# Retention and two feed-forward layers on one Trainium2 core: two first-block products are computed inside the retention, with earlier slice conversion, a paired last group and an output scale spread by TensorE

## The chip, the cores and the metric

The kernel runs as one program on one core of a Trainium2 chip. The metric is the device time of one execution in microseconds; a smaller number is better. The engines are named as in the profile: PE is TensorE's matmul (PEld its weight load), DVE is VectorE, ACT is ScalarE, POOL is GpSimd, SP is SyncE, which issues most loads.

## The reference

Three steps follow each other. A retention: for each of 4 batches and 8 heads a state of 64 x 64 runs over 768 tokens,

```
state = gamma[h] * state + outer(k[t], v[t])
y[t]  = (1 / sqrt(64)) * (q[t] @ state)
```

Then y becomes x of 3072 tokens by 512, and two feed-forward layers with 2048 hidden units follow: `h = x @ w_in; x = (h * sigmoid(1.702 * h)) @ w_out`, and `h = x @ w_in2; out = relu(h)**2 @ w_out2`. Weights arrive as float64 words and are brought to pairs of float32 parts (a high part that TensorE multiplies in one pass, and a low part, the rest).

## The kernel before

**The retention.** The 3072 tokens are cut into 24 units of 128 (6 per batch). Unit u has two loads of 512 KB (`load_unit`, issued on SP, line 459; the second one is half as long for the last unit of a batch). Seven units are in flight; the load of unit u + 7 is issued when unit u's outputs are done. The work goes in groups, line 477: units 0 to 3 one by one, then pairs (4, 5) to (20, 21), then 22 and 23 one by one, so k runs from 0 to 15 with an empty last group. In the loop at line 632 each group k does, in program order:

- `scores` of its units (line 487, PE): products of q and k, 8 float32 products per unit, into the PSUM tags `sc0` or `sc1`, with the scaled v of the unit on POOL (line 504, `vs`);
- ScalarE's high part of a converted weight slice, if one is held (`cv_high`, line 163), and ScalarE's high part of x for the first block (`split_0`, line 516);
- `outputs` of group k - 1: `grow` adds to the state in `dp` (line 552), which ScalarE copies out (line 557); `within` (line 566) and `across` (line 581) give the outputs in PSUM tag `yp` (or `sc1` for units 1 and 22);
- DVE: the masks of group k (line 496, `pt`), the low part of x for the first block, in `cv_group` the low part of the held slice (line 168) and in groups 8, 10, 12, 14 the conversion of another one (`convert`: lines 142 and 148), and last `scaled`, the scaling of the outputs of group k - 1 by the table `ytab` (lines 603, 610, 613);
- POOL's issues of slice loads (`cv_load`, line 128, in groups 5, 7, 9, 10, 12, ...), ScalarE's scaling of a loaded slice (`cv_a`, line 136), and the loads of later units.

The scores of group k + 1 need the score bank that the masks of group k read; `within` needs the masks, and the `yp` bank that `scaled` of the group before has read. `sc0`, `sc1` and `yp` are one buffer of two banks each, `dp` two banks. Each engine works through its own list in order.

The output scale of batch chunk 0, `ytab_sb[0]`, is a load of 128 x 512 float32 (256 KB) on SP's queue between the two halves of unit 2 (line 627); ScalarE derives the other five from it (line 645). Ahead of unit 0 TensorE runs 9 warm-up products (line 475), behind unit 0's scores 6 more (`fill`, line 637).

**The first layer, first two blocks of 512 tokens.** For n = 0, 1 the loop at line 853 runs over 16 slices f: `up(n, f)` is 12 matmuls of 128 x 512 (lines 675 to 677) into PSUM tag `b{f % 4}`, then Gelu and a high copy on ScalarE (lines 684, 685) and the low part on DVE (line 689); `down(n, f - 2)` is 12 more into `b4` to `b7` (lines 712 to 714). During block 0 each `up` also converts 2, 2, 2 or 3 weight slices (`cv_step`), each with a high copy, a rounding and a low part, until all 32 are done. The PSUM pool `ps` of this stage (line 665) is opened when the retention's pool closes, and each of its tiles waits for the earlier tile in the same place (`reuse_waits="tile"`).

**The rest** runs the second half of the tokens and the second layer with a seven-product scheme for 2 x 2 blocks (line 893), for which `background` prepares weights on DVE, ScalarE and POOL; the change touches none of it.

Of the kernel before, what the change touches and what calls it, by code (L numbers as in the profile page):

```python
# [10 lines left out]
F32 = mybir.dt.float32  # L11
F32R = mybir.dt.float32r
# [3 lines left out]
ACTF = mybir.ActivationFunctionType  # L16
# [3 lines left out]
P = 128  # L20
# [25 lines left out]
BG0 = 4.5  # L46
BG1 = (4.9,) * 9 + (2.6,) * 5 + (2.8, 0.0)
PAUSE = 3.0
CVG = (8, 10, 12, 14)
RAWG = {5: 1, 7: 1, 9: 1, 10: 1, 12: 1, 13: 2, 14: 1, 15: 1}  # L50
FILL = 6
RAWS = 5
BGUP = (2.4, 2.75)
BGD = (0.6, 1.9)
# [11 lines left out]
def tile_retention_then_two_ffns(  # L66
# [90 lines left out]

    held = deque()

    def cv_high():  # L160
        if held:
            w, hm, key = held[0]
            nc.scalar.copy(out=w[:, :, 0], in_=hm.rearrange("p (k c) -> p k c", c=P))

    def cv_low():
        if held:
            w, hm, key = held.popleft()
            v.tensor_tensor(
                out=w[:, :, 1], in0=hm.rearrange("p (k c) -> p k c", c=P), in1=w[:, :, 0], op=ALU.subtract
            )  # L170
            ws[key] = w
# [13 lines left out]
    def cv_group(k):  # L185

        cv["step"] += 1
        cv_low()
        if k in CVG and cv["b"] < cv["a"]:
            convert()  # L190

    def cv_ahead(k):

        if k == CVG[-1] - 1:
            cv["ahead"] = RAWS
        for _ in range(RAWG.get(k, 0)):
            cv_load()
        n = cv["a"]
        if n < min(cv["load"], cv["b"] + 2) and cv["step"] >= loaded[n] + 2:
            cv_a()  # L200

    def cv_step(f=None):

# [213 lines left out]
    def split_x(n, src, t=None):  # L417
# [5 lines left out]
            v.tensor_tensor(out=lo, in0=x, in1=hi, op=ALU.subtract)  # L423
        hl[n] = t

    with tc.manual_schedule():

        with (
# [30 lines left out]
                    nc.sync.dma_start(out=units[u][i][:, a - 1024 * i:z - 1024 * i], in_=qkv[u, :, a:z])  # L459

            nc.scalar.dma_start(out=tab_sb, in_=tab)
            load_unit(0)
            warm_sb = att.tile([P, 512], BF16, tag="x0", name="warm_sb")
            nc.vector.memset(warm_sb, 0.0)
# [9 lines left out]
            for i in range(WARM):  # L474
                nc.tensor.matmul(warm[:, 0, :, :], warm_sb[:, 0:P], warm_sb, start=True, stop=True)

            groups = [(u,) for u in range(4)] + [(u, u + 1) for u in range(4, NU - 2, 2)] + [(NU - 2,), (NU - 1,)]
            second = {pair[1] for pair in groups if len(pair) > 1}

            def scores(u):  # L480
# [29 lines left out]
            def split_0():  # L510
# [14 lines left out]

                return low if blocks else None

            def banked(t):
                return t.rearrange("p (k b) i -> p b k i", b=2)

            def outputs(pair):

                tag = "sc1" if pair in ((1,), (NU - 2,)) else "yp"
                yp = aps.tile([P, 2, NP, P], F32, tag=tag, name=f"yp{pair[0]}", bufs=1)

                def views(u):
# [4 lines left out]
                def grow(u):  # L541

                    b, c = divmod(u, CPB)
                    if c == CPB - 1:
                        return
                    kn = views(u)[1]
                    vs = pend[u][1]
                    dp = state[b][0] if c else aps.tile([P, NP, D], F32, tag="dp", name=f"dp{b}")
                    for p in range(NP):
                        for a in range(2):  # L550
                            h = 2 * p + (a ^ p % 2)
                            nc.tensor.matmul(  # L552
                                dp[64 * a:64 * a + 64, p, :], kn[:, h, :], vs[:, h, :],
                                start=(c == 0 and p == 0), stop=(c == CPB - 2), skip_group_check=True,
                            )
                    ns = att.tile([P, NP, D], F32, tag="st", name=f"st{u}", bufs=3)
                    nc.scalar.copy(out=ns, in_=dp)
                    state[b] = (dp, ns)
                    snaps[u + 1] = ns
# [63 lines left out]
                return scaled  # L623

            load_unit(1)
            load_unit(2, (0, 1024))
            nc.sync.dma_start(out=ytab_sb[0], in_=ytab)
            load_unit(2, (1024, 2048))
            for u in range(3, UNITS):
                load_unit(u)  # L630

            for k, group in enumerate(groups + [()]):
                masks = [scores(u) for u in group]
                if k == 0:
                    fill = aps.tile([P, 2, NP, P], F32, tag="yp", name="fill", bufs=1)
                    for i in range(FILL):
                        nc.tensor.matmul(fill[:, 0, :, :], warm_sb[:, 0:P], warm_sb, start=True, stop=True)
                cv_high()
                low = split_0()
                before = groups[k - 1] if k > 0 else ()  # L640
                scaled = outputs(before) if before else None
                for u in group:
                    if 0 < u < CPB:
                        for p in range(NP):
                            nc.scalar.mul(ytab_sb[u][:, p, :], ytab_sb[0][:, p, :], ystep_sb[:, u, p:p + 1])
                for masked in masks:
                    masked()
                if low is not None:
                    low()
                cv_group(k)  # L650
                if scaled is not None:
                    scaled()
                cv_ahead(k)
                for u in before:
                    load_unit(u + UNITS)
# [8 lines left out]
            wpool[f] = wb_p  # L664
        ps_p = ctx.enter_context(tc.tile_pool(name="ps", bufs=1, space=PSUM, reuse_waits="tile"))

        gs = {}
        acc = {}

        def up(n, f):  # L670
            hi, lo = weights(f, 0)
            hp = ps_p.tile([P, TB], F32, tag=f"b{f % 4}", name=f"h{n}_{f}")
            for k in range(KD):
                xh, xl = hl[n][k]
                nc.tensor.matmul(hp, lo[:, k], xh, start=(k == 0), stop=False)  # L675
                nc.tensor.matmul(hp, hi[:, k], xh, start=False, stop=False)  # L676
                nc.tensor.matmul(hp, hi[:, k], xl, start=False, stop=(k == KD - 1))  # L677
            slots = [wr_p[i] for i in (EARLY, EARLY + 1 + 2 * (f % 2), EARLY + 2 + 2 * (f % 2))]
            g, gh, gl = (
                pool.tile([P, TB], t, tag="w", name=f"{name}{n}_{f}")  # L680
                for pool, t, name in zip(slots, (F32, F32R, F32R), ("gs", "gh", "gl"))
            )

            nc.scalar.activation(out=g, in_=hp, func=ACTF.Gelu_apprx_sigmoid)
            nc.scalar.copy(out=gh, in_=g)
            gs[n, f] = (gh, gl)

            def low():
                v.tensor_tensor(out=gl, in0=g, in1=gh, op=ALU.subtract)

            if n == 0 and cv["b"] < len(order):
                cv_step(low)
                for _ in range(1 + (f % 4 == 3)):
                    if cv["b"] < len(order):
                        cv_step()
            else:
                low()
                if n == NSTD - 1:
                    next(first_x, None)
                pace(n, f)  # L700
# [150 lines left out]
            fetch()  # L851

        for n in range(NSTD):
            for f in range(NF):
                up(n, f)
                if f >= LOOK:
                    down(n, f - LOOK)
# [285 lines left out]
def _tables():  # L1143
# [4 lines left out]
    vt = np.exp(-t[:, None] * lg[None, :]).reshape(CPB, P, H).transpose(1, 0, 2).reshape(P, CPB * H)  # L1148

    yt = np.exp(t[:P, None] * lg[None, :]) / np.sqrt(D)  # L1150
    yt = np.repeat(yt.reshape(P, NP, 2).transpose(2, 1, 0), D, axis=0)

    ys = np.exp(P * np.arange(CPB)[:, None] * lg[None, :])
    ys = np.repeat(ys.reshape(CPB, NP, 2).transpose(2, 0, 1).reshape(2, CPB * NP), D, axis=0)
# [69 lines left out]
```

## Time and profile before

| | us |
|---|---|
| median of 3 runs | 1023.68 (1023.49 to 1024.23) |
| profiled execution, its own time | 1023.72 |
| its span, first to last instruction | 1022.0 |
| PE busy | 1012.6 (99%) |
| DVE busy | 734.0 (72%) |
| ACT busy | 525.5 (51%) |
| POOL busy | 143.9 (14%) |
| retention: start to the first slice product | 80.70 |

The span is what the profile covers; the execution's own time is 1.7 us longer. PE is busy nearly all the time, so the waits of PE are what is left to look for, and the place to look is the retention, where its matmuls are short and depend on loads, masks and scalings. Busy shares of the other engines say only how much of their time is spoken for, not whether PE waits for them.

### The profile page before, as it was taken

Reading aid. Unit: us, or ns where it says so; the run is one execution under the profiler, and the core shown is the slowest. Engines: PE = TensorE matmul, PEld = TensorE weight load, DVE = VectorE, ACT = ScalarE, POOL = GpSimd, SP = SyncE. Lnnn points to the kernel's source line nnn. Section 1 sums busy time; section 2 is a strip of 40 time slices with the busy share of each in tenths; the row PEclk is TensorE's granted clock in tenths of the full one; section 3 lists DMA queues with packets and bytes.
Section 4 is the critical chain, followed back from the end, with each engine's and each line's share of the span. In section 5 each row is a group of like instructions: output and inputs, shape, how many; then the busy total and the mean of one; then the engine's idle time right before and its main releaser. Section 6 shows DMA issues by size and latency. Waiting matters only on the chain.

```text
span 1022.0 us, 15448 instructions
## 1 busy us (share of the span) xinstructions
PE 1012.6 (99%) x5551; PEld 838.4 (82%) x5551; DVE 734.0 (72%) x976; ACT 525.5 (51%) x815; POOL 143.9 (14%) x209
## 2 busy tenths in 40 slices
PE   8999999999999999999999999999999999999998
PEld 6988888888888888888888888888888888888886
DVE  5778897997566998566998576885455985446953
ACT  4126765444556565556565787563234463334433
POOL 2442222431111101211102210001000001000000
PEclk9999999999999999999999999999999999999999
DMA  9995766995999978999978999867766867766664
GB/s 354 407 368 179 277 226 253 363 362 209 372 358 356 334 270 271 405 377 351 349 249 271 399 401 306 273 209 240 211 194 194 275 213 246 204 194 195 211 191 144
DMA packets 119627, 287.65 MB, mean 281 GB/s; under 512 B 13056, under 2 KB 13184, under 8 KB 119296
## 3 DMA queue, kind: packets, MB, share of 16 engines
q1 hardware_dynamic: 90864, 181.71, 52.8%
q0 software_dynamic: 27968, 103.82, 27.7%
q10 hardware_dynamic: 720, 1.15, 0.3%
q8 instruction: 44, 0.72, 0.3%
q14 instruction: 31, 0.25, 0.1%
HBM read 213.23 MB, written 73.40 MB: 280 GB/s over the span
## 4 chain that ended last, share of the span: by engine, by line
PE 96%; DMA 2%; DVE 1%; ACT 0%; issue 0%; SPq 0%
PE D L893 37%; PE X L893 21%; PE Z L893 10%; PE Y L893 5%; PE h L675 3%; PE y L712 3%; PE h L677 3%; PE y L714 3%; PE h L676 3%; PE y L713 3%; DMA unit<-qkv 2%; PE yp L566 2%; PE sc L487 2%; PE yp L581 1%; PE dp L552 1%; DMA tab_sb<-tab 0%
## 5 line engine op out<-in xcount | busy, mean ns | idle before, releaser
L893 PE MATMUL D<-gx,r 128*128 128x512 f32 x1680 | 383.2, 389 | 0.0
L893 PEld LDWEIGHTS D<-gx,r 128*128 128x128 f32 x1680 | 314.9, 188 | 66.7 <-DVE gx L1012 1.4
L1012 DVE TENSOR_TENSOR gx<-g,gx 128x1024 fp32r<-128x1024 f32 x140 | 170.4, 1220 | 44.7 <-ACT gx L1011 44.2
L893 PE MATMUL X<-xh,r 128*128 128x512 f32 x640 | 197.3, 389 | 0.2 <-ACT g L911 0.2
L1011 ACT CAST gx<-g 128x1024 fp32r<-128x1024 f32 x140 | 145.5, 1051 | 89.8 <-PE D L893 83.0
L911 ACT COPY g<-X 128x512 f32<-128x512 f32 x120 | 70.1, 584 | 176.9 <-PE X L893 176.9
L916 DVE TENSOR_TENSOR g<-Z,g 128x512 f32<-128x512 f32 x80 | 55.1, 689 | 132.9 <-ACT g L911 98.2
L893 PEld LDWEIGHTS X<-xh,r 128*128 128x128 f32 x640 | 120.0, 188 | 25.7 <-ACT g L911 0.8
L893 PE MATMUL X<-xl,r 128*128 128x512 f32 x320 | 124.5, 389 | 0.0
L893 PE MATMUL Z<-xh,r 128*128 128x512 f32 x320 | 98.5, 389 | 0.0
L893 PEld LDWEIGHTS Z<-xh,r 128*128 128x128 f32 x320 | 60.1, 188 | 12.5
L893 PEld LDWEIGHTS X<-xl,r 128*128 128x128 f32 x320 | 60.1, 188 | 12.5
L893 PE MATMUL Z<-xl,r 128*128 128x512 f32 x160 | 62.2, 389 | 0.0
L336 POOL DMA_DIRECT2D kw<-wq x32 | 30.2, 944 | 196.9 <-DVE wq L335 144.0
L136 ACT ACTIVATE raw<-raw 128x384 f32<-128x384 f32 (+1 forms) x96 | 46.0, 514 | 8.5 <-DMA raw<-w 8.5
L675 PE MATMUL h<-hl,w 128*128 128x512 f32 x128 | 49.9, 390 | 0.0
L676 PE MATMUL h<-hl,w 128*128 128x512 f32 x128 | 49.8, 389 | 0.0
L677 PE MATMUL h<-hl,w 128*128 128x512 f32 x128 | 49.8, 389 | 0.0
L712 PE MATMUL y<-gh,w 128*128 128x512 f32 x128 | 49.8, 389 | 0.0
L713 PE MATMUL y<-gh,w 128*128 128x512 f32 x128 | 49.8, 389 | 0.0
L714 PE MATMUL y<-gl,w 128*128 128x512 f32 x128 | 49.8, 389 | 0.0
L893 PE MATMUL Y<-xh,r 128*128 128x512 f32 x160 | 49.3, 389 | 0.0
(100 smaller groups left out, 1354.2 us busy)
## 6 DMA issues: line engine op xcount, KB each, us to landing
r<-kw SPq DMA_DIRECT2D x560, 256.0 KB, 3.5
kw<-wq POOLq DMA_DIRECT2D x32, 896.0 KB, 7.3
unit<-qkv SPq DMA_DIRECT2D x44, 512.0 KB, 9.9
raw<-w POOLq DMA_DIRECT2D x32, 512.0 KB, 5.2
kw<-wh POOLq DMA_DIRECT2D x16, 1024.0 KB, 5.9
raw<-win POOLq DMA_DIRECT2D x16, 512.0 KB, 7.8
kw<-w POOLq DMA_DIRECT2D x16, 512.0 KB, 6.8
raw<-wout POOLq DMA_DIRECT2D x16, 512.0 KB, 8.8
```

The costliest lines, as they stand in the source:

```text
L136: nc.scalar.activation(out=hm[:, a:z], in_=raw[:, a:z, 1].bitcast(F32), func=ACTF.Prelu, scale=scale, alpha=-2.0 ** 32)
L675: nc.tensor.matmul(hp, lo[:, k], xh, start=(k == 0), stop=False)
L676: nc.tensor.matmul(hp, hi[:, k], xh, start=False, stop=False)
L677: nc.tensor.matmul(hp, hi[:, k], xl, start=False, stop=(k == KD - 1))
L712: nc.tensor.matmul(a, lo[:, e], gh, start=s0, stop=False)
L713: nc.tensor.matmul(a, hi[:, e], gh, start=False, stop=False)
L714: nc.tensor.matmul(a, hi[:, e], gl, start=False, stop=s1)
L893: nc.tensor.matmul(a, w, b, start=start, stop=stop, skip_group_check=True)
L911: nc.scalar.copy(out=t, in_=a)
L916: v.tensor_tensor(out=t, in0=a, in1=t, op=ALU.add)
L1011: nc.scalar.copy(out=hi, in_=src)
L1012: v.tensor_tensor(out=lo, in0=src, in1=hi, op=ALU.subtract)
```

## The change

- The output scale comes as 2 rows (a 2 x 128 selector beside the 2 x 512 scale, loaded on ScalarE's queue behind the mask table) and one product of TensorE in place of the six fill products spreads it over the partitions; ScalarE copies it out of PSUM. The 256 KB load on SP goes, and unit 2 is loaded like the others.
- Units 22 and 23 become a pair, so the retention has 14 groups and the empty one. The outputs of this last pair go to tag `sc0`.
- Slice loads begin in group 7 instead of 5; conversions are 1, 1, 2, 1, 2, 1 in groups 9 to 14 instead of one in groups 8, 10, 12 and 14, and nine slices are scaled by ScalarE within the retention. The high and low parts of held slices are made at the head of the group, ahead of the masks.
- In groups 10 and 11 the products of slices 0 and 1 of block 0 (`early_up`) run between the scores and the outputs, with Gelu, high copy and low part; the low part stands on DVE behind the masks and ahead of the conversions. `dp` has one bank, the product `hp` has the other.
- Block 0's loop starts at slice 2, and converts 2, 3, 2, 3, ... slices per `up`.

```diff
-CVG = (8, 10, 12, 14)
-RAWG = {5: 1, 7: 1, 9: 1, 10: 1, 12: 1, 13: 2, 14: 1, 15: 1}
-FILL = 6
+CVG = {9: 1, 10: 1, 11: 2, 12: 1, 13: 2, 14: 1, 15: 1}
+RAWG = {7: 1, 8: 1, 9: 2, 10: 1, 11: 2, 12: 2, 13: 2, 14: 1}
+EARLYUP = {10: 0, 11: 1}
...
         cv["step"] += 1
-        cv_low()
-        if k in CVG and cv["b"] < cv["a"]:
-            convert()
+        for _ in range(CVG.get(k, 0)):
+            if cv["b"] < cv["a"]:
+                convert()
...
-        if k == CVG[-1] - 1:
+        if k == 9:
             cv["ahead"] = RAWS
         for _ in range(RAWG.get(k, 0)):
             cv_load()
-        n = cv["a"]
-        if n < min(cv["load"], cv["b"] + 2) and cv["step"] >= loaded[n] + 2:
-            cv_a()
+        for _ in range(CVG.get(k + 1, 0)):
+            n = cv["a"]
+            if n < cv["load"] and cv["step"] > loaded[n]:
+                cv_a()
...
+    def product(hp, hi, lo, x):
+        for k in range(KD):
+            xh, xl = x[k]
+            nc.tensor.matmul(hp, lo[:, k], xh, start=(k == 0), stop=False)
+            nc.tensor.matmul(hp, hi[:, k], xh, start=False, stop=False)
+            nc.tensor.matmul(hp, hi[:, k], xl, start=False, stop=(k == KD - 1))
...
             nc.scalar.dma_start(out=tab_sb, in_=tab)
+            ysel = xy_p.tile([P, 2, TB], F32, tag="xy", name="ysel").rearrange("p a n -> p (a n)")[0:2, 0:P + NP * P]
+            nc.scalar.dma_start(out=ysel, in_=ytab)
...
-            groups = [(u,) for u in range(4)] + [(u, u + 1) for u in range(4, NU - 2, 2)] + [(NU - 2,), (NU - 1,)]
+            groups = [(u,) for u in range(4)] + [(u, u + 1) for u in range(4, NU, 2)]
...
+            def early_up(f):
+
+                if not spare:
+                    spare.append(wa_p.tile([P, 2, TB], F32, tag="w1", name="ge"))
+                hp = aps.tile([P, TB], F32, tag="hp", name=f"h0_{f}", bufs=1)
+                product(hp, *weights(f, 0), hl[0])
+                g = spare[0][:, f]
+                t = wa_p.tile([P, 2, TB], F32R, tag="w1", name=f"ghl{f}")
+                nc.scalar.activation(out=g, in_=hp, func=ACTF.Gelu_apprx_sigmoid)
+                nc.scalar.copy(out=t[:, 0], in_=g)
+                gs[0, f] = t[:, 0], t[:, 1]
+                return lambda: v.tensor_tensor(out=t[:, 1], in0=g, in1=t[:, 0], op=ALU.subtract)
...
-                tag = "sc1" if pair in ((1,), (NU - 2,)) else "yp"
+                tag = {(1,): "sc1", groups[-1]: "sc0"}.get(pair, "yp")
...
-            load_unit(2, (0, 1024))
-            nc.sync.dma_start(out=ytab_sb[0], in_=ytab)
-            load_unit(2, (1024, 2048))
-            for u in range(3, UNITS):
+            for u in range(2, UNITS):
                 load_unit(u)
...
-                    for i in range(FILL):
-                        nc.tensor.matmul(fill[:, 0, :, :], warm_sb[:, 0:P], warm_sb, start=True, stop=True)
-                cv_high()
+                    nc.tensor.matmul(fill[:, 1, :, :], ysel[:, 0:P], ysel[:, P:], start=True, stop=True)
+                    nc.scalar.copy(out=ytab_sb[0], in_=fill[:, 1, :, :])
+                for i in range(len(held)):
+                    cv_high(i)
+                while held:
+                    cv_low()
                 low = split_0()
+                if k in EARLYUP:
+                    low = early_up(EARLYUP[k])
...
-                for _ in range(1 + (f % 4 == 3)):
+                for _ in range(1 + f % 2):
...
-            for f in range(NF):
+            for f in range(0 if n else LOOK, NF):
```

## Rows read from the trace of the kernel before

**Rows 1.** Waits of PE: line, what for, us in total, times, longest:

```profile
PE sc L487 <- DMA unit<-qkv: 2.2, 3, 1.3
...
PE yp L581 <- issue: 1.0, 2, 0.6
```

**Rows 2.** Windows: PE, PEld, DVE, ACT, POOL busy, PE clock, DMA share, GB/s:

```profile
20.00:40.00 20.00, 18.76 (x368) 17.02 (x370) 13.56 (x25) 4.99 (x17) 8.65 (x11) 1.00 1.03 407
...
66.00:81.00 15.00, 15.00 (x316) 13.42 (x313) 12.69 (x18) 4.74 (x10) 5.93 (x8) 1.00 0.61 225
81.00:160.00 79.00, 79.00 (x350) 65.37 (x349) 68.01 (x117) 50.06 (x87) 19.63 (x34) 1.00 0.67 231
```

**Rows 3.** Chain that ended last, in the retention: start us, us, what:

```profile
26.32 0.61 PE dp L552 x16
...
29.71 1.99 PE sc L487 x32
...
57.87 0.60 issue
...
59.22 1.99 PE sc L487 x32
...
72.03 0.61 PE dp L552 x16
...
75.90 1.09 PE sc L487 x16
```

**Rows 4.** Timeline of PE up to unit 11: start us, us, and idle before:

```profile
1.20 4.02 PE L475 MATMUL warm<-warm_sb 128*128 128x512 bf16 x9 [1.20 <-DVE warm_sb L464]
...
6.41 1.47 PE L637 MATMUL fill<-warm_sb 128*128 128x512 bf16 x6
...
25.16 1.16 PE L487 MATMUL sc<-unit 64*128 64x128 f32 x16 [0.62 <-DMA unit<-qkv]
...
35.05 1.16 PE L487 MATMUL sc<-unit 64*128 64x128 f32 x16
36.65 1.16 PE L487 MATMUL sc<-unit 64*128 64x128 f32 x16 [0.43 <-DVE x L603]
```

**Rows 5.** The same chain at the first matmuls of slices 0, 1 and 2:

```profile
80.70 0.43 PE h L675
...
83.69 0.23 PE h L675
...
86.41 0.23 PE h L675
```

**Rows 6.** Timeline of DVE and POOL in groups 6, 10, 12 and 13:

```profile
31.12 2.34 DVE L496 TENSOR_TENSOR pt<-sc,tab_sb 128x1024 f32<-128x1024 f32 x2
...
53.87 2.34 DVE L496 TENSOR_TENSOR pt<-sc,tab_sb 128x1024 f32<-128x1024 f32 x2
...
69.02 1.19 POOL L504 TENSOR_TENSOR vs<-unit,tab_sb 128x512 f32<-128x512 f32 x1 [1.46 <-DVE pt L496]
69.34 1.46 DVE L148 SCALAR_TENSOR_TENSOR hm<-raw,hm 128x512 uint16<-128x512 uint16 x1
...
70.86 1.29 DVE L610 TENSOR_TENSOR xout<-yp,ytab 128x512 f32<-128x512 f32 x2
```

**Rows 7.** DVE's groups by form, 0 to 82 us: busy us, mean ns:

```profile
L148 DVE SCALAR_TENSOR_TENSOR hm<-raw,hm 128x512 uint16<-128x512 uint16 x5 | 4.5, 890 | 0.2
...
L168 DVE TENSOR_TENSOR w<-hm,w 128x512 fp32r<-128x512 f32 x4 | 2.7, 683 | 0.1
L142 DVE TENSOR_SCALAR hm<-raw 128x512 uint32<-128x512 uint32 x5 | 2.1, 418 | 0.0
```

**Rows 8.** Timeline of DVE and ACT at the end of the retention:

```profile
80.80 0.68 DVE L610 TENSOR_TENSOR xout<-yp,ytab 128x512 f32<-128x512 f32 x1
...
84.43 0.62 ACT L685 CAST gh<-gs 128x512 fp32r<-128x512 f32 x1
85.09 0.69 DVE L689 TENSOR_TENSOR gl<-gs,gh 128x512 fp32r<-128x512 f32 x1 [2.49 <-ACT gh L685]
```

More of the change, by code (lines that the diff above doesn't have):

```diff
@@ L158, in tile_retention_then_two_ffns, with cv_high @@
     held = deque()
-    def cv_high():
+    def cv_high(i=0):
         if held:
-            w, hm, key = held[0]
+            w, hm, key = held[i]
             nc.scalar.copy(out=w[:, :, 0], in_=hm.rearrange("p (k c) -> p k c", c=P))
@@ L424, in split_x @@
         hl[n] = t
+    gs = {}
+    def product(hp, hi, lo, x):
[4 more added lines that the diff above has]
+            nc.tensor.matmul(hp, hi[:, k], xl, start=False, stop=(k == KD - 1))
     with tc.manual_schedule():
@@ L526, in split_0 @@
                 return low if blocks else None
+            spare = []
+            def early_up(f):
[9 more added lines that the diff above has]
+                return lambda: v.tensor_tensor(out=t[:, 1], in0=g, in1=t[:, 0], op=ALU.subtract)
             def banked(t):
@@ L547, in grow @@
                     vs = pend[u][1]
-                    dp = state[b][0] if c else aps.tile([P, NP, D], F32, tag="dp", name=f"dp{b}")
+                    dp = state[b][0] if c else aps.tile([P, NP, D], F32, tag="dp", name=f"dp{b}", bufs=1)
                     for p in range(NP):
@@ L665, in tile_retention_then_two_ffns @@
         ps_p = ctx.enter_context(tc.tile_pool(name="ps", bufs=1, space=PSUM, reuse_waits="tile"))
-        gs = {}
         acc = {}
@@ L672, in up @@
             hp = ps_p.tile([P, TB], F32, tag=f"b{f % 4}", name=f"h{n}_{f}")
[L673 to L677, printed above, removed]
+            product(hp, hi, lo, hl[n])
             slots = [wr_p[i] for i in (EARLY, EARLY + 1 + 2 * (f % 2), EARLY + 2 + 2 * (f % 2))]
@@ L1150, in _tables @@
     yt = np.exp(t[:P, None] * lg[None, :]) / np.sqrt(D)
-    yt = np.repeat(yt.reshape(P, NP, 2).transpose(2, 1, 0), D, axis=0)
+    yt = yt.reshape(P, NP, 2).transpose(2, 1, 0).reshape(2, NP * P)
+    yt = np.concatenate([np.repeat(np.eye(2), D, axis=1), yt], axis=1)
     ys = np.exp(P * np.arange(CPB)[:, None] * lg[None, :])
```

## Prediction

> **What bounds the kernel now.** The page's head comes first: PE is busy 99% of 1022.0 us. Then the waits of TensorE: in the whole run it loses 2.2 us to unit loads and 1.0 us to two "issue" gaps [rows 1], 1.2 us at the start, and little else. So no later stage can get faster by better feeding, and the change takes no matmul away there: 24 matmuls of slices 0 and 1 only move forward. Only what PE loses before its first slice product at 80.70 us can be won, and a new wait of PE anywhere is lost for good, since no slack behind it takes it up. The windows come next: from 20 to 40 us DMA runs at a share of 1.03 and PE's row shows 18.76 of 20 us; from 66 to 81 us PE shows no gap, while DVE is at 12.69 of 15 us [rows 2]. In the timeline the last wait of PE that is plainly a load's ends with the scores of unit 7 at 25.16 us [rows 4], and from there the chain of waits is PE almost throughout. So the retention is bound by loads up to 25 us and by PE after that, with DVE not far behind. That last point decides my forecast.
>
> **The change part by part.**
>
> *Output scale from two rows.* The 256 KB load of the scale stood on SP's queue between the halves of unit 2. It goes, and all later units land sooner by 262 KB at 407 GB/s [rows 2], 0.64 us. The gap that this can close is PE's wait of 0.62 us for unit 7 [rows 4]. Gain 0.62. The small load that replaces it stands on ScalarE's queue behind the mask table's and is due at 6.5 us. The selector product takes at the dearest two 512-column passes (each float32 product of the scores leaves two records) of 0.245 us, as the six fill products ran [rows 4]. It takes their place ahead of PE's wait for unit 1, which hides it as it hid them; without that cover it would cost 0.5 us. ScalarE's copy out of PSUM (about 0.6 us) ends near 8 us, before the first use. Joining unit 2's halves changes no byte.
>
> *Slice loads from the eighth group.* Before, the first slice's load was issued in group 5, among those of units 8 to 11, and the scores of unit 11 start 1.60 us after those of unit 10 [rows 4] instead of 1.00, half a pair's 1.99 [rows 3]. The row names a VectorE operation, but the score bank that this would free had its masks read by 33.46 [rows 6]; the load of unit 11 is the likely cause, so 0.60 us more is won. Together 1.22. Later there are nine slice loads instead of five ahead of unit 23, 524 KB each (1.3 us at 407 GB/s). PE is then some 5.5 us later through the two products, which is what four more loads take: nothing, and a rival below. POOL issues them behind the multiplies of their group; the next group's multiplies wait for their units longer than that. The two stores of `xout` come sooner after the retention, ahead of slice loads on POOL's queue; five converted slices lie in between: nothing.
>
> *Two products in the retention.* The first twelve matmuls ran from 80.70 to 83.69, 2.99 us, the next twelve from 83.69 to 86.41, 2.72 us [rows 5]. Moved, they cost what they save, but the change from short to long matmuls (0.27) comes twice more: 0.5. Each also starts with the low part of a slice that DVE now makes at the head of the group, behind the scaling of the group before. In group 10 that scaling ended at 53.87, where the masks began [rows 6]; plus 0.68 for the low part [rows 7] it is ready 0.3 us after the scores end at about 54.3. Twice 0.3. ScalarE's Gelu and copy (about 0.6 each) stand ahead of the group's state copies, whose results PE needs only after a pair of `within` products (1.75): nothing.
>
> *Pairing units 22 and 23.* From 72.03 to 80.70 [rows 3, 5], 8.67 us, PE did the outputs of 20 and 21 (3.87, to 75.90), one unit's scores and two single outputs. As a pair these are 3.87, 1.00 and 3.39 (26.32 to 29.71 [rows 3]), 8.26. Gain 0.4, if PE sets the end.
>
> *DVE's queue.* Four conversions become eight, each of 0.42 + 0.75 and a low part of 0.68 [rows 7] (0.75: the five roundings without the one of 1.46), with two low parts of the products (0.69) [rows 8]. Masks of a pair take 2.34, its scaling 1.29 [rows 6]. In groups 10 and 11 the product's low part stands on DVE ahead of conversions and scaling, and waits for ScalarE; from the end of the product to its start it took 1.40 us (83.69 to 85.09) [rows 5, 8]. From there DVE has no slack. In groups 11 to 14 it must do one such low part (0.69), six conversions (7.02), five slice low parts (3.40), two pairs of masks (4.68) and four scalings (5.16): 20.95 us. PE needs for the same stretch three pairs of outputs at 3.4 to 3.9, a last one at 3.39 and two pairs of scores at 1.99, about 18.5 us, and starts 1.4 us sooner. So DVE ends the retention about 4 us behind PE.
>
> *Why that lag reaches PE.* The outputs of 22 and 23 now go to the bank pair `sc0`, the first that its pool takes (banks 0 and 1). In the program of before the next pool gave its banks in the order of first use: b0, b1, b2, then b4 to b7, then b3 are banks 0 to 7. After the change the first use is slice 2's product, `b2`, which by that order gets bank 0, and the last reader of that is DVE's scaling of 22 and 23, the last item of its queue. Before, that reader was harmless: slice 0 started at 80.70 [rows 5] while the scaling of unit 23 ran, in another bank, from 80.80 [rows 8].
>
> *The sum.* The scores of 18 and 19 end at 59.22 + 1.99 = 61.21 [rows 3]. Less 1.22, plus 2 x 0.3, plus 2 x 2.99: the second product ends at 66.57. Plus 1.40, DVE starts at 67.97; plus 20.95 and an estimated 0.1 for the release, slice 2 starts at 89.02. It started at 86.41 [rows 5]. So 2.6 us slower. The issue gap of 0.60 at 57.87 [rows 3] lies in the sum and may not come again: 2.0; without the 0.5 for the change of matmuls 1.5. One rounding took 1.46 us, beside a POOL multiply that had begun before it [rows 6]; the mean of five is 0.89 [rows 7], so 0.14 more for each of six would make it 3.4; with an early gain of only 0.62, 4.0. Own range 1.5 to 4.0.
>
> *Elsewhere.* The first block's conversions go 2, 3, 2, 3 per slice for 24 slices instead of 28. PE is busy 79.0 of 79.0 us there and DVE 68.0 [rows 2], and PE's order leaves each slice five conversions ahead of need: nothing. One `dp` bank instead of two: the next batch's state starts a group after the last read of the old one: nothing.
>
> **The rivals.**
> *Forecast, slower by 2.6* (0.48, of which 0.44 over the bound below).
> *No change* (0.30): the bank is another, or DVE catches up. Then PE sets the end: -1.22 - 0.4 + 0.6 + 0.5 = -0.5, and with PE waiting for DVE inside (the outputs of 20 and 21 for the scaling of 18 and 19, some 0.6, a state copy, 0.3) +0.4: 1022.9 to 1024.4. For it: DVE's durations are those of single rows. Against it: both steps above.
> *Faster* (0.14): that, and the issue gaps (1.0) and the waits for low parts (0.6) go too: -2.1, 1021.6. For it: the gaps lie where DMA is full. Against it: later it is fuller.
> *The port* (0.02): if POOL's multiplies held back each of six conversions as they did one, by 0.71, that makes 4.3 more: 1030.6. Against it: one of five was held back. The Trainium skill ("SBUF — State Buffer", Who interferes with whom) says that VectorE and GpSimd share a port pair, and that the later one is blocked for all of the other's instruction. By that rule each conversion that meets a multiply pays; the trace agrees for the one that did, 1.46 beside 0.75.
> *Loads late* (0.04): nine slice loads hold back units 22 and 23; each that is not covered is 1.3 us, from the point where unit 23 lands later than the scores of 22 end. Two give 1026.3. Against it: 5.5 us more of PE time.
> *The clock falls* (0.02): without the fill PE idles about 1.2 us before unit 1. The granted clock reads 1.00 in the windows [rows 2], yet the nine warm-up products took 0.447 us each and the fill 0.245 [rows 4], so the start ran at about half of what came after. Half speed once more for the 4.02 us of the warm-up would cost up to 2 us on top of the forecast. The Trainium skill ("TensorE: Matmul & The Clock Gate", What's actually happening) has half rate as the default and activity as what lifts it. By that rule the gap counts against the change; no row here has such a gap.
>
> **How the numbers follow.** The profiled execution took 1023.72 us, 0.04 over the median of 1023.68. Some 0.2%, 2.05 us, is what can be told from no change. Slower: 0.44 + 0.02 + 0.04 + 0.02 = 0.52. Same: 0.04 of the forecast + 0.30 = 0.34. Faster: 0.14. Time: 1023.7 + 2.6 = 1026.3. The range goes from a little below no change, 1022.2, leaving most of the faster case out, to the forecast's upper end, 1027.7.
>
> **What would show it.** Right: slice 2's first matmul waits 2 to 4 us, between 85 and 90 us, for the last scaling of `xout`; DVE shows almost no gap from group 11 on; the waits for units 7 and 11 shrink. Wrong: that matmul follows the last output without a gap, or DVE idles in groups 12 to 14, or PE waits for unit 22 or 23.

## The result: 1029.6 us, 5.8 us slower

| | before | after |
|---|---|---|
| median | 1023.79 us (1023.49 to 1024.23) | 1029.61 us (1028.80 to 1030.87) |
| ratio | 1 | 1.0058, interval 1.0040 to 1.0075 |
| profiled execution | 1023.72 us, span 1022.0 | 1029.46 us, span 1027.7 |

The direction and the place of the loss are as forecast; the size is not: 5.8 us instead of 2.6, and above the range. In the waits of PE after the change, the first row is the one forecast. The second, PE held up by DVE's scalings inside the retention, stood only in the rival of no change, with some 0.6 us. The last is one that the forecast did not have. The loads' row answers to [rows 1] (2.2 us there), and the issue gaps of [rows 1] are gone. Of the four executions behind the median that of 1028.80 us had a mean granted clock of 1.000, those of 1029.46 (the profiled one), 1029.76 and 1030.87 us 0.998, 0.998 and 0.997, so the low clock described below does not come every time.

```profile
PE h L432 <- DVE xout L637: 2.9, 1, 2.9
PE yp L593 <- DVE xout L637: 1.8, 2, 1.1
PE sc L499 <- DMA unit<-qkv: 1.6, 3, 0.7
...
PE D L917 <- DVE gx L1036: 1.1, 2, 0.5
```

**Up to slice 2.** PE's timeline (start, duration, instruction, idle before it in brackets). The scores of units 12 and 13 start at 40.10 us; in the trace of before they started at 41.60. The two early products begin at 53.41 and 62.47.

```profile
40.10 2.06 PE L499 MATMUL sc<-unit 64*128 64x128 f32 x32
...
53.41 0.50 PE L432 MATMUL h<-hl,w 128*128 128x512 f32 x1
...
62.47 0.50 PE L432 MATMUL h<-hl,w 128*128 128x512 f32 x1 [0.18 <-DVE w L168]
...
84.73 1.10 PE L608 MATMUL yp<-unit,st 64*64 64x128 f32 x32
88.69 0.60 PE L432 MATMUL h<-hl,w 128*128 128x512 f32 x1 [2.86 <-DVE xout L637]
89.09 0.63 PE L433 MATMUL h<-hl,w 128*128 128x512 f32 x1
...
93.10 0.40 PE L736 MATMUL y<-ghl,w 128*128 128x512 f32 x1
```

DVE's timeline: the low part of the second product starts at 66.86, and the scaling of units 22 and 23, for which slice 2 waits, ends at 87.27 + 1.28 = 88.55.

```profile
66.86 0.69 DVE L553 TENSOR_TENSOR ghl<-ge,ghl 128x512 fp32r<-128x512 f32 x1 [2.19 <-ACT ghl L551]
67.47 1.27 DVE L142 TENSOR_SCALAR hm<-raw 128x512 uint32<-128x512 uint32 x1
68.77 1.46 DVE L148 SCALAR_TENSOR_TENSOR hm<-raw,hm 128x512 uint16<-128x512 uint16 x1
...
84.98 1.29 DVE L168 TENSOR_TENSOR w<-hm,w 128x512 fp32r<-128x512 f32 x2
86.18 0.42 DVE L142 TENSOR_SCALAR hm<-raw 128x512 uint32<-128x512 uint32 x1
86.64 0.73 DVE L148 SCALAR_TENSOR_TENSOR hm<-raw,hm 128x512 uint16<-128x512 uint16 x1
87.27 1.28 DVE L637 TENSOR_TENSOR xout<-yp,ytab 128x512 f32<-128x512 f32 x2
```

**Behind that wait.** The windows (columns as in [rows 2]): DVE at 14.03 of 15 us where [rows 2] had 12.69, PE idle from 86 to 88, and then a granted clock of 0.50, which is the lower of its two levels.

```profile
66.00:81.00 15.00, 13.16 (x270) 12.12 (x267) 14.03 (x18) 5.65 (x12) 6.29 (x7) 1.00 0.75 285
...
86.00:88.00 2.00, 0.00 (x0) 0.00 (x0) 1.97 (x5) 0.00 (x0) 0.08 (x1) 1.00 0.69 221
88.00:90.00 2.00, 1.31 (x4) 1.05 (x5) 1.62 (x3) 0.00 (x0) 0.45 (x1) 0.72 0.67 227
90.00:92.00 2.00, 2.00 (x6) 1.60 (x5) 0.00 (x0) 0.00 (x0) 0.53 (x1) 0.50 0.65 236
92.00:94.00 2.00, 2.00 (x9) 1.61 (x8) 0.00 (x0) 0.60 (x1) 0.00 (x0) 0.93 0.49 188
```

PE's timeline of before at the start of slice 2:

```profile
86.24 0.39 PE L675 MATMUL h<-hl,w 128*128 128x512 f32 x1
```

So the 5.7 us between the two profiled executions come in three steps. Slice 2 starts at 88.69; the timeline of before had it at 86.24 (the chain of [rows 5] 86.41): **2.45 us**. Its twelve matmuls then take 93.10 - 88.69 = 4.41 us to the next instruction, 2.72 in [rows 5]: **1.69 us**, since they follow each other 0.43 us apart while the clock is at 0.50 and 0.23 apart at 1.00. By 375 us the distance between the two traces has grown by another 0.8 us, and by the end to 5.73; these last **1.6 us** are small waits of PE, the longest at 374, 527 and 528 us, in a stage that the diff does not touch.

### The profile page after: what moved, and what is told of

It reads as the page before. It is cut to its first block, busy times and chain, and to the rows that moved or that the text cites. A ratio compares the mean times of both kernels' runs of the same rounds, so it can differ in the third digit from the quotient of the medians.

```text
span 1027.7 us, 15429 instructions
## 1 busy us (share of the span) xinstructions
PE 1014.9 (99%) x5547; PEld 839.8 (82%) x5547; DVE 734.4 (71%) x976; ACT 525.9 (51%) x816; POOL 145.2 (14%) x209
## 4 chain that ended last, share of the span: by engine, by line
PE 90%; DMA 5%; DVE 3%; ACT 1%; issue 1%; SPq 0%; POOL 0%; POOLq 0%; DVEq 0%; ACTq 0%
PE D L917 36%; PE X L917 21%; PE Z L917 11%; PE Y L917 5%; DMA unit<-qkv 5%; PE h L432 3%; PE y L738 3%; PE y L736 3%; PE y L737 3%; PE h L433 3%; PE h L434 3%; ACT xh L759 1%; DVE hm L142 0%; DVE pt L508 0%; DVE xout L637 0%
## 5 line engine op out<-in xcount | busy, mean ns | idle before, releaser
L432 PE MATMUL h<-hl,w 128*128 128x512 f32 x128 | 50.7, 396 | 3.0 <-DVE xout L637 2.9
L433 PE MATMUL h<-hl,w 128*128 128x512 f32 x128 | 50.5, 395 | 0.0
L434 PE MATMUL h<-hl,w 128*128 128x512 f32 x128 | 50.4, 394 | 0.0
L336 DVE TENSOR_TENSOR wq<-w,wq 128x896 fp32r<-128x896 f32 x32 | 34.8, 1088 | 19.2 <-ACT wq L370 19.2
L736 PE MATMUL y<-gh,w 128*128 128x512 f32 x120 | 46.7, 389 | 0.0
L737 PE MATMUL y<-gh,w 128*128 128x512 f32 x120 | 46.7, 389 | 0.0
L738 PE MATMUL y<-gl,w 128*128 128x512 f32 x120 | 46.7, 389 | 0.0
```

The costliest lines, as they stand in the source:

```text
L336: v.tensor_tensor(out=t[:, :, 1], in0=w[:, 1:8], in1=t[:, :, 0], op=ALU.subtract)
L736: nc.tensor.matmul(a, lo[:, e], gh, start=s0, stop=False)
L737: nc.tensor.matmul(a, hi[:, e], gh, start=False, stop=False)
L738: nc.tensor.matmul(a, hi[:, e], gl, start=False, stop=s1)
```

## The experiments

Twelve kernels ran, each beside the kernel before on the same chip, whose medians there were 1023.9 to 1024.1 us. Behind each median stands the range of its executions, behind each ratio to the kernel before its 95% interval; the diffs are excerpts, with `...` where lines are left out. The first three take one step each out of the changed kernel.

### The bank of slice 2

```diff
+        acc[0] = [ps_p.tile([P, TB], F32, tag=f"b{4 + e}", name=f"y0_{e}") for e in range(KD)]
         for n in range(NSTD):
...
-            if s0:
+            if s0 and n > 0:
                 acc[n] = [ps_p.tile(...) for e in range(KD)]
```

> The changed kernel, but the four banks of the first block's sums are taken before slice 2's product, so that this product gets a bank that the masks of unit 23 read (free at 81.7 us) and the sums get the first four. Theory (slice 2 waits only for the bank that the last scaling reads): it follows the last output at about 85.8 us with no wait of 2.9 us, the clock stays at 1.00, and of the 5.8 us that the change costs 3.1 of wait and 1.7 of half speed go: about 1025.0 us, plus up to 0.2 for the first sum, whose bank the scaling still holds at 88.5. Rival (PE waits for VectorE's lag in whatever bank, for a low part or a copy): the wait moves to the next product, 1028 to 1030 us.

Measured: **1025.30 us** (1025.02 to 1027.15), ratio to before 1.0014 (1.0005 to 1.0023). With another bank, slice 2 follows the last outputs without a wait, though DVE's work is the same; the clock stays at 1.00. PE's timeline:

```profile
85.16 1.10 PE L608 MATMUL yp<-unit,st 64*64 64x128 f32 x32
86.19 0.50 PE L432 MATMUL h<-hl,w 128*128 128x512 f32 x1
```

The wait and the slow stretch behind it are gone, 4.3 us; the waits at 374 to 528 us are still there (`PE D L918 <- DVE gx L1037` again 1.1 us in its waits). So the wait is on the bank, as forecast, and without it the clock does not fall here; that an idle PE brings it down is left to the third experiment.

### The conversions of the first block

```diff
-                for _ in range(1 + f % 2):
+                for _ in range(1 + (f % 4 == 3)):
```

> The changed kernel, but the first block converts 2, 3, 2, 2 slices per product, as the kernel before did, so that the last conversion falls into slice 12 again and the preparation of the later weights starts as late as before. Theory (the 1.6 us that PE loses between 374 and 528 us come from the preparation starting one slice sooner): these waits go back to those of the kernel before, about 1028.0 us. Rival (they come from the shift of 4 us itself, or from chance): 1029.0 to 1030 us with the waits at the same places.

Measured: **1027.87 us** (1026.43 to 1028.55), 1.0036 (1.0023 to 1.0049): 1.7 us less than the change, with the wait of 2.9 us and the low clock behind it still there. The waits for `gx` are gone from PE's list. What was late is seen near 370 us. The changed kernel, PE's row that waits, and DVE's timeline ahead of it:

```profile
374.48 1.88 PE L917 MATMUL D<-gx,r 128*128 128x512 f32 x7 [0.53 <-DVE gx L1036]
```

```profile
369.62 1.09 DVE L336 TENSOR_TENSOR wq<-w,wq 128x896 fp32r<-128x896 f32 x1
370.62 1.22 DVE L764 TENSOR_TENSOR xl<-xb,xh 128x1024 fp32r<-128x1024 f32 x1
373.20 1.23 DVE L1036 TENSOR_TENSOR gx<-g,gx 128x1024 fp32r<-128x1024 f32 x1 [1.36 <-ACT gx L1035]
```

DVE's timeline of this kernel in the same place:

```profile
369.63 0.28 DVE L367 TENSOR_TENSOR w<-w 128x128 f32<-128x128 f32 x1
369.95 0.29 DVE L368 TENSOR_TENSOR w<-w 128x128 f32<-128x128 f32 x1
370.16 1.22 DVE L764 TENSOR_TENSOR xl<-xb,xh 128x1024 fp32r<-128x1024 f32 x1
372.63 1.23 DVE L1036 TENSOR_TENSOR gx<-g,gx 128x1024 fp32r<-128x1024 f32 x1 [1.26 <-ACT gx L1035]
```

Ahead of `xl` the changed kernel runs a step of the background preparation of 1.09 us, this kernel two of 0.28 and 0.29. `xl` comes 0.46 us later, the next `gx` 0.57, and PE waits 0.53. By the code, eight conversions in the retention and 2, 3, 2, 3 per slice end the conversions in slice 11 instead of 12, and the preparation starts a slice earlier; from then on each of its steps lies beside other work than it was set out for. In this kernel's trace no other loss is left: slice 2 starts at 88.83, 2.59 us later than before, and with 1.7 for the clock that is the 4.3 us between the two spans (1026.3 and 1022.0).

### PE kept busy through the wait

```diff
+                if not group:
+                    busy = aps.tile([P, TB], F32, tag="hp", name="busy", bufs=1)
+                    hi, lo = weights(0, 0)
+                    for i in range(10):
+                        nc.tensor.matmul(busy, hi[:, i % KD], hl[0][i % KD][0], start=True, stop=True)
```

> The changed kernel with ten extra products of 512 columns, whose result nobody reads, in PE's wait behind the last outputs (2.3 of its 2.9 us). Theory (the clock fell because PE was idle in this wait): slice 2 still starts at about 88.7 us, its matmuls take 0.23 us each instead of 0.43, the clock reads 1.00 from there, about 1027.9 us. Rival (the clock falls for what PE does before, its many short matmuls and smaller waits from 70 us on): half speed stays, 1029 to 1030 us.

Measured: **1028.19 us** (1027.99 to 1028.97), 1.0043 (1.0031 to 1.0056). Slice 2 starts nearly as late, but at the full clock, 1.00 in the window from 88 to 90 us, so it was the idle PE that brought the clock down. The instruction behind slice 2's twelve matmuls starts at 91.10, 2.84 us after slice 2 instead of 4.41: the clock's part by itself is 1.6 us in the trace. The whole time is 1.4 us less. That is not the clock alone: slice 2 also starts 0.43 sooner, and by the end some 0.6 us of the sum is lost again. PE's timeline, then the window:

```profile
85.33 2.56 PE L675 MATMUL busy<-hl,w 128*128 128x512 f32 x10
88.26 0.47 PE L432 MATMUL h<-hl,w 128*128 128x512 f32 x1 [0.37 <-DVE xout L637]
```

```profile
88.00:90.00 2.00, 1.74 (x8) 1.46 (x9) 1.19 (x3) 0.00 (x0) 0.25 (x2) 1.00 0.67 219
```

### The last scaling first

In the last, empty group the two low parts and the conversion go behind the scaling (`held` and `cv_group` move behind `scaled()`); bank 0 stays.

```diff
+                if group:
+                    cv_group(k)
                 if scaled is not None:
                     scaled()
+                if not group:
+                    for i in range(len(held)):
+                        cv_high(i)
+                    while held:
+                        cv_low()
+                    cv_group(k)
```

> The changed kernel; in the last group of the retention VectorE does the scaling of units 22 and 23 first, and the two held low parts and the conversion after it. Slice 2 keeps bank 0. Theory (the wait is VectorE's queue standing ahead of the last scaling): the scaling runs at about 86 to 87 us, slice 2 starts at about 87.3 instead of 88.69, its wait is 1 to 1.9 us instead of 2.9; with the clock still falling behind it 1028.2 us, with the clock at 1.00 about 1026.5. The waits of some 1.6 us late in the run stay. Rival (the wait is set by something other than the order of VectorE's queue): slice 2 at 88.5 to 88.9 and 1029.6 us.

Measured: **1026.61 us** (1026.32 to 1027.56), 1.0025 (1.0015 to 1.0034). The two values of the expectation were 1028.2 and 1026.5 by the clock; it stayed at 1.00. PE's timeline, then DVE's, then the window:

```profile
84.62 1.10 PE L608 MATMUL yp<-unit,st 64*64 64x128 f32 x32
87.23 0.47 PE L432 MATMUL h<-hl,w 128*128 128x512 f32 x1 [1.50 <-DVE xout L637]
```

```profile
85.80 1.29 DVE L637 TENSOR_TENSOR xout<-yp,ytab 128x512 f32<-128x512 f32 x2 [0.83 <-PE yp L608]
```

```profile
88.00:90.00 2.00, 2.00 (x10) 1.69 (x9) 1.93 (x5) 0.00 (x0) 0.05 (x1) 1.00 0.15 59
```

DVE now waits 0.83 us for the outputs, so in this order it is no longer behind PE: 1.4 of the 2.9 us were the three items ahead of the scaling in its queue, and the other 1.5 are the scaling itself and its release, which only another bank avoids. Half of the wait is gone, and the clock's part with it: 3.0 us less than the change.

### Both repairs

The first two edits together.

> Both repairs on the changed kernel: the other banks for slice 2 (as in e1_banks, 1025.3 us) and 2, 3, 2, 2 conversions per slice (as in e2_conv). Theory (the two losses are independent): the late waits of 1.9 us that e1_banks still has go, about 1023.4 us, 0.6 faster than the kernel before. Rival (the late waits of e1_banks come from its own timing): 1025 us stays.

Measured: **1023.92 us** (1023.14 to 1024.78), 0.9998 (0.9989 to 1.0007). The two parts nearly add up (4.3 and 1.7 against 5.7). Nothing is won either: slice 2 starts at 85.78, 0.46 us ahead of before, and the end of the profiled run is 0.2 us ahead. One cost of the change is left that neither repair touches, PE's waits for DVE's scalings inside the retention:

```profile
PE yp L593 <- DVE xout L637: 1.8, 2, 1.1
```

### Four conversions instead of eight

The changed kernel, with four conversions in groups 9, 10, 12 and 14 and the rest in the slices.

```diff
-CVG = {9: 1, 10: 1, 11: 2, 12: 1, 13: 2, 14: 1, 15: 1}
+CVG = {9: 1, 10: 1, 12: 1, 14: 1, 15: 1}
...
-                for _ in range(1 + f % 2):
+                for _ in range(1 + (f % 2 == 1 or f == 12)):
```

> The changed kernel, slice 2 still in the bank of the last scaling, but four conversions in the retention instead of eight (groups 9, 10, 12, 14), the other four in the first block, so that the last one again falls into slice 12. Theory (the size of slice 2's wait is VectorE's lag from conversions): VectorE has 7.4 us less to do, the lag is gone, slice 2 waits only for the scaling that follows the last output, 1.5 us instead of 2.9, and starts near 85.5 us; the clock stays; about 1023 us. Rival (the lag comes from the products' low parts, which stand ahead of the scaling): the wait stays near 2.9 us with half speed behind it, about 1027.9 us.

Measured: **1057.36 us** (1055.34 to 1059.34), 1.0323 (1.0309 to 1.0337): both readings were far off. Now PE waits for the slices themselves, for slice 2 too (2.10 us, to 86.60), and the clock falls again and again (waits of PE):

```profile
PE h L432 <- DVE w L168: 20.8, 8, 3.7
```

The two early products put PE two slices ahead, and with four conversions fewer the slices are not ready for it. So, with the block's conversions in this order, the work on DVE that makes slice 2 late is what the early products need.

### Parts of the change on the kernel before

The scale from two rows and the selector product, without the six fill products:

```diff
-            nc.sync.dma_start(out=ytab_sb[0], in_=ytab)
...
-                    for i in range(FILL):
-                        nc.tensor.matmul(fill[:, 0, :, :], ...)
+                    nc.tensor.matmul(fill[:, 1, :, :], ysel[:, 0:P], ysel[:, P:], start=True, stop=True)
+                    nc.scalar.copy(out=ytab_sb[0], in_=fill[:, 1, :, :])
```

> The kernel before with one part of the change alone: the output scale from two rows, the selector product in place of the six fill products, no 256 KB load among the units. Theory (all units land 0.6 us sooner and the retention is bound by loads up to 25 us): unit 7's wait of 0.62 us goes, 0.6 us faster, about 1023.1 us. Rival (the selector product at half speed, or the missing fill, costs what the load gave): 1023.6 to 1025 us.

Measured: **1023.73 us** (1023.19 to 1024.42), 0.9996 (0.9987 to 1.0005). The scores of unit 6 start at 22.77 us instead of 23.37, which is the 0.6 forecast, and slice 0 only 0.15 earlier (80.48 for 80.63): issue gaps of PE in between took it back. In this trace the clock falls at the start, as a window shows:

```profile
8.00:10.00 2.00, 2.00 (x16) 1.78 (x16) 0.00 (x0) 0.19 (x1) 0.62 (x1) 0.50 1.03 332
```

The missing fill alone does not decide that: of the ten traces without the fill in its old place the clock falls there in three (this one and those of the second and third experiments) and stays at 1.00 in seven, that of the change among them. A cost does not show in the traces: the scores of unit 6 come at 22.77 us here, and at 22.80 in the kernel of 1022.49 us below, whose clock stayed at 1.00. The times leave one open: the three executions with a mean granted clock of 0.998 took 1023.82 to 1024.42 us, the six with 1.000 took 1023.19 to 1023.94.

The pair of units 22 and 23 alone (its outputs in `sc1`):

```diff
-            groups = ... + [(u, u + 1) for u in range(4, NU - 2, 2)] + [(NU - 2,), (NU - 1,)]
+            groups = ... + [(u, u + 1) for u in range(4, NU, 2)]
```

> The kernel before, with units 22 and 23 as one group at the end (their outputs in the bank pair sc1); nothing else of the change. Theory (as in the prediction's term for the pair): 0.4 us less up to slice 0, 1023.6 us. Rival (VectorE's masks and scalings of a pair come in a lump and TensorE or slice 0 waits for them): no gain or a loss of up to 1 us, 1024 to 1025 us.

Measured: **1023.97 us** (1023.57 to 1024.33), 0.9998 (0.9989 to 1.0006). In the trace slice 0 starts at 80.20 instead of 80.63, the 0.4 us forecast; at slice 2 0.2 are left of it and at the end 0.1. In the times it does not show.

The later slice loads alone:

```diff
-CVG = (8, 10, 12, 14)
-RAWG = {5: 1, 7: 1, 9: 1, 10: 1, 12: 1, 13: 2, 14: 1, 15: 1}
+CVG = (10, 12, 14, 15)
+RAWG = {7: 1, 9: 1, 10: 1, 12: 1, 13: 1, 14: 2, 15: 1}
```

> The kernel before, with the first slice load two groups later (group 7 instead of 5) and its four conversions in groups 10, 12, 14 and 15; nothing else of the change. Theory (as in the prediction's term for the loads): the scores of unit 11 no longer come 0.6 us late, 1023.4 us. Rival (that wait is covered by a later one, or the load was not its cause): 1023.8 to 1024.2 us.

Measured: **1023.38 us** (1023.05 to 1024.32), 0.9993 (0.9984 to 1.0002): the median is the theory's, but the interval holds no change too, and the profiled execution is one of the slower ones (1024.30 us). From the scores of unit 10 to those of unit 12 it is 5.85 us (35.28 to 41.13) instead of 6.55 (35.05 to 41.60), so the load was the cause of unit 11's wait; but slice 0 is at 80.66, where it was.

### The early part without the early products

The changed kernel without the two early products, with all eight conversions, another bank for slice 2 (the first experiment's edit), `range(f > 0)` for the conversions of the block and its loop from slice 0:

```diff
-EARLYUP = {10: 0, 11: 1}
+EARLYUP = {}
```

> The changed kernel without the two products in the retention (slices 0 and 1 go up at the head of the first block again), eight conversions in the retention, sums' banks taken first as in e1_banks, conversions ending in slice 12. Theory (PE has no time to spare in the retention, the products win nothing, but they give VectorE 5.5 us to catch up): PE's waits for VectorE in groups 12 to 14 grow from 1.8 us, but the 0.5 for changing between short and long matmuls and the low parts' waits go: within 0.7 of e5_banks_conv, 1023 to 1024 us. Rival (the products fill real holes of PE): 1.5 us or more slower than e5_banks_conv.

Measured: **1027.91 us** (1026.01 to 1029.88), 1.0034 (1.0022 to 1.0047). The rival reading came true: without the products it is 4.0 us slower than with them (1023.92), so they fill real holes of PE. The late loads of the prediction's list appear, but only where the products are gone (waits of PE, then its timeline):

```profile
PE sc L499 <- DMA unit<-qkv: 4.3, 7, 1.8
PE sc L499 <- issue: 1.5, 1, 1.5
PE yp L608 <- issue: 1.3, 1, 1.3
```

```profile
74.55 1.16 PE L499 MATMUL sc<-unit 64*128 64x128 f32 x16 [1.78 <-DMA unit<-qkv]
```

The nine slice loads come ahead of units that PE now reaches sooner; the row is unit 23. Of the 4.3 us, 2.3 lie ahead of 40 us, as in the other kernels, so the late loads are 2.0 us; the two issue gaps are 2.8, and their cause is open. Slice 0 starts at 82.90. The trace is of the fastest of five executions (1026.01 us), so 1.9 us of the median are not in it. In the changed kernel the time of the two products covers these loads, as the prediction had it.

The same with four conversions and seven slice loads in groups 7 to 14 (`CVG = {9: 1, 11: 1, 13: 1, 14: 1, 15: 1}`), which leaves the scale, the later loads and the pair:

> As e7_noearly with only four conversions in the retention (groups 9, 11, 13, 14): what is left of the change is the scale from two rows, the later slice loads and the paired last group. Theory (VectorE does not bind then, and these three parts are the gain of the change): unit loads 1.5 us sooner by group 8, pairing 0.4, about 1022.1 us, the fastest so far. Rival (loads or issue gaps take the place of what is won): 1023.3 to 1024 us.

Measured: **1022.49 us** (1022.16 to 1023.92), ratio 0.9987 (0.9978 to 0.9996), the best of all. Slice 0 starts 2.1 us sooner than before, and PE waits for loads 1.9 us and for issue 0.6. PE's timeline:

```profile
77.50 1.10 PE L608 MATMUL yp<-unit,st 64*64 64x128 f32 x32
78.54 0.50 PE L432 MATMUL h<-hl,w 128*128 128x512 f32 x1
```

And with the six fill products put back behind the selector product:

```diff
                     nc.scalar.copy(out=ytab_sb[0], in_=fill[:, 1, :, :])
+                    for i in range(6):
+                        nc.tensor.matmul(fill[:, 0, :, :], warm_sb[:, 0:P], warm_sb, start=True, stop=True)
```

> The kernel before with the output scale from two rows, the slice loads from group 7 on, four conversions in groups 9, 11, 13 and 14 and units 22 and 23 as one group (which took 1022.5 us), and now the six fill products kept ahead of unit 1. Theory (the fill only keeps the clock up at the start, where the loads bind): the clock does not fall at about 8 us, and the time stays within 0.4 us of 1022.5. Rival (the half clock at the start costs time): 1021.5 us or less.

Measured: **1023.79 us** (1022.91 to 1025.09), 0.9994 (0.9985 to 1.0002); neither reading fits. In this place the fill waits 0.67 us for ScalarE's copy and then runs at the low clock, which lasts from 8.2 to 11.6 us here, while in the trace of the kernel without the fill it stayed at 1.00 (PE's timeline):

```profile
8.39 2.72 PE L663 MATMUL fill<-warm_sb 128*128 128x512 bf16 x6 [0.67 <-ACT ytab L661]
```

The scores of unit 1 come at 11.04 us instead of 8.18 in the kernel without it, those of units 12 and 13 still 0.75 later. The profiled execution took 1024.58 us; the three with a mean granted clock of 1.000 took 1022.91 to 1023.79. It does not settle what a fill in its old place would do.

## Why the prediction was right about the place and wrong about the size

**Right: the bank and the lag.** "Slice 2's first matmul waits 2 to 4 us, between 85 and 90 us, for the last scaling of `xout`": 2.86 us, to 88.69, where 89.02 was forecast. Another bank removes it, and the low clock with it. The other signs came too: DVE has no gap from 66.86 to 88.55, the wait for unit 7 is 0.31 instead of 0.62 us, and that for unit 11 is gone.

**Its terms.** The retention got 1.5 us ahead by group 8 (1.22 forecast). The early products cost what was said, the wait for their low parts 0.2 once instead of 0.3 twice, and the issue gap of 0.60 did not come again. So DVE began its last stretch at 66.86 instead of 67.97, and had 88.55 - 66.86 = 21.7 us to do instead of 20.95. The excess is in the conversions. By DVE's groups by form from 66 to 89 us, against the mean of 418 ns in [rows 7] and the single rounding of 0.75:

```profile
L148 DVE SCALAR_TENSOR_TENSOR hm<-raw,hm 128x512 uint16<-128x512 uint16 x7 | 5.9, 849 | 0.2
...
L142 DVE TENSOR_SCALAR hm<-raw 128x512 uint32<-128x512 uint32 x7 | 4.4, 622 | 0.0
```

Line 142 took 7 x 0.20 = 1.4 us more for its seven and line 148 0.7 more (the seventh conversion lies behind the scaling and took no longer than in [rows 7], so this is the excess of the six in the sum); starts that follow a little closer than the durations, as 66.86 to 67.47 for a duration of 0.69, gave part of it back. The two errors, 1.1 sooner and 0.7 longer, nearly cancel, so that 88.69 lies so near to 89.02 is partly luck.

**Wrong: the sum ended at the start of slice 2.** It took every matmul behind the wait at its old pace. In the profiled execution the wait of 2.9 us also brought the clock down to 0.50, from 88.9 to 92.3 us: 1.7 us. The rival of the falling clock was in the list, but at the start of the kernel, with 0.02; it was never put behind the very wait that the forecast itself added.

**Wrong: "Elsewhere ... nothing".** The sentence gave PE's slices their conversions five ahead, and that held: no wait for a slice in the first block. But it asked only who waits for the conversions, not what starts when they end. That cost 1.6 us, near 300 us later and beyond, shown by the second experiment. The 1.7 and the 1.6 together are what the forecast of 2.6 us lacks.

**The rivals.** No change is what the kernel with both repairs does (1023.92 us, within its 1022.9 to 1024.4). Late loads appeared only without the products. Conversions beside GpSimd's multiplies did get longer, the first step more than the rounding, but by 2.1 us in all, not 4.3. Faster did not happen with the early products in any version; without them it did, by 1.4 us. Why the gains of the early part shrink is seen in part: PE waits 1.1 to 2.0 us for DVE's scalings inside the retention wherever the early products and eight conversions stay, and issue gaps of PE of up to 1.5 us come in other places in other versions. What makes the gaps was not settled, and whether early products could ever pay was not tried beyond these kernels.

## What to carry to other kernels

Price a new wait of TensorE with what the clock may do behind it: here a wait of 2.9 us cost 4.3, and one of 1.5 us 1.3. When work that is done ahead ends sooner than before, look at what starts on its end; background work set out against another engine's schedule shifts as a whole. And before work is pulled forward, list who reads last in the bank that the next product gets, and put that reader at the head of its queue or the product in another bank.

## What the runs showed of the hardware

- **The clock.** It fell to 0.50 behind waits of 2.86 us (the change) and 2.85 (the second experiment), and stayed at 1.00 behind one of 1.50 (the last scaling first). The length of the wait alone does not tell: in the kernel of 1057 us it stayed at 1.00 behind the first wait for a slice, of 2.10 us, and fell behind or at the end of each of the next six, of 1.92, 2.86, 3.72, 3.73, 1.87 and 3.73 us (PE's timeline and the window behind the wait of 1.92):

```profile
94.25 0.50 PE L432 MATMUL h<-hl,w 128*128 128x512 f32 x1 [1.92 <-DVE w L168]
```

```profile
96.00:98.00 2.00, 2.00 (x6) 1.58 (x5) 0.00 (x0) 0.00 (x0) 0.39 (x1) 0.50 0.97 365
```

  The Trainium skill ("TensorE: Matmul & The Clock Gate", What's actually happening) has the low rate as the default and activity as what lifts it; the trace of the change agrees, 0.50 behind the idle stretch and 1.00 again from 92.3 us with PE at work. In the second experiment the fall came only at 90.0 us, when PE had been working again since 88.83 (PE's timeline, then the windows):

```profile
88.83 0.47 PE L432 MATMUL h<-hl,w 128*128 128x512 f32 x1 [2.85 <-DVE xout L637]
```

```profile
88.00:90.00 2.00, 1.17 (x5) 1.02 (x6) 1.78 (x4) 0.00 (x0) 0.53 (x1) 1.00 0.60 201
90.00:92.00 2.00, 2.00 (x6) 1.53 (x6) 0.00 (x0) 0.00 (x0) 0.53 (x1) 0.50 0.63 199
```

- **Conversions beside GpSimd.** A conversion's first step (`L142`, 0.42 us alone) took 1.27 and the rounding after it 1.46 while GpSimd's multiplies ran from 67.15 for 2.49 us (the changed kernel's timeline of POOL). In that trace each first step or rounding from 45 to 89 us that began while a multiply ran took 1.00 to 1.46 us, each other one 0.41 to 0.42 or 0.73 to 0.76. No run took the multiplies away, but in the third experiment one came later, at 76.71 us, and the first step at 76.03 took 0.42 us, where the changed kernel's at 75.88, beside a multiply from 75.56 on, took 1.00. The Trainium skill ("SBUF — State Buffer", Who interferes with whom) has the two engines share a port pair; these traces agree with it.

```profile
67.15 2.49 POOL L516 TENSOR_TENSOR vs<-unit,tab_sb 128x512 f32<-128x512 f32 x2 [2.67 <-PE yp L593]
```

- **A low clock whose cost does not show in the trace.** At half rate from 7.9 to 11.3 us the kernel with the new scale alone still had the scores of unit 6 at 22.77 us; a wait for a load that the lost time can go into, 1.32 us ahead of unit 5 in the trace of before, is nearly gone there. Its times by execution leave a cost of some 0.5 us open.
